# Stacked float32r products for a low rank term, one-step value ends and products of ones in a planned TensorE stream

## The chip, the cores and the metric

The kernel runs on one core of a Trainium2 chip. The metric is the time of one execution on the device, in microseconds (us). Three runs of the kernel before took 713.5, 714.14 and 715.22 us; the median is 714.14. The profile is of one further execution.

## The reference

Four sequences of 576 tokens go through three blocks, all in float32. Cut to what matters:

```
# 1: windowed attention, 8 heads of 64
scores = where(0 <= i-j < 128, q k^T/8 - slope_h |i-j|, -1e9);  x = softmax(scores) v   # (4, 576, 512)
# 2: low rank mixing of tokens, then a wide layer over channels
h = x^T @ U @ V                  # U: 576 x 32, V: 32 x 576, for each sequence
u = x + h^T
x = u + relu(u @ w_ch1) @ w_ch2  # 512 -> 2048 -> 512
# 3: gated unit
h = relu(x @ w_in);  a, v = halves of h (512 each)
v_n = (v - mean(v)) / sqrt(var(v) + 1e-6)
v_s = w_spatial @ v_n + b_spatial       # mixes the 576 tokens
out = (a * v_s) @ w_out
```

The inputs `U`, `V` and the weights are float64 in memory and are brought to float32 bit by bit in the kernel.

## The kernel before, in words

Nothing in the kernel is issued in the order of the source text. Every step is a `Task` with an engine (or several to choose from), an estimated cost, a due time and the buffer parts that it reads and writes. `Plan.run` lays all tasks out in a simulated time line eight times, each time with due times worked out backwards from the layout before, keeps the layout that ends first, and emits the instructions in that order. So the order on each engine's queue is fixed before the launch, and a changed cost or task anywhere may change the order everywhere. Buffers are slots of rings; two rings may name the same slot, and a later user of a slot waits for the earlier one. Semaphores come from these uses.

**Exact products.** TensorE multiplies float32r operands in one pass, float32 operands in two recorded passes. Where float32 accuracy is wanted at the float32r rate, an operand is split in a float32r high part and a float32r remainder, and a product becomes three: high by high, low by high, high by low. The wide layers use this (lines 545 to 547, 584 to 586, 885 to 887, 1421 to 1423 and others).

**Front.** The four sequences' attention comes first (`heads`, a task group for each pair of heads): scores (line 1044), maximum and bias on VectorE (1055), exponentials on ScalarE (1060), scaling on VectorE or GpSimd (1082), transposes (1090), products with the values (1128). Sequence 0 is scaled after the products (`plain`). Between these tasks the planner sets the first quarter of the wide layer (`early_group`, lines 545 to 586), as soon as its tokens are ready. `turn_over` (991) issues products of a 128 by 128 tile of ones (`hot`) before the first scores.

**Low rank term.** `turned` transposes a sequence's `u` (1155). `low_rank` mixes the tokens with `U` into a PSUM tile `t` whose strip of 32 partitions number `pair` holds the 32 mixed rows of that pair of heads (1171). A copy brings `t` to SBUF as `th`; then `up` makes, for each half of 288 tokens, one float32 product per pair on that pair's strip of 32 rows of the array: 32 rows of `th` against the same strip of `v32`, which holds `V` four times, one copy for each strip (1184). VectorE adds each result to `u` (1189). Sequence 0 does this in two calls of `low_rank` for two pairs each, the other sequences in one for all four.

**Values.** In the third block (`values_of`) the tokens are taken in tiles of 128, of which the first 64 tokens of two sequences b and b+1 share one (c = 0, in every even sequence). Its normalised rows must stand as two tiles `ends`, where rows 64i to 64i+63 belong to sequence i: `ends[0]` holds twice the first 32 tokens, `ends[1]` twice the next 32. Line 1476 normalises 32 rows at a time into each end and line 1479 doubles them on ScalarE. The edge operands of the token mixing (`value_forms`, 1506) read them, and the last product of each sum (1577) uses these. Line 1593 adds the sums.

## Time and profile before

| | |
|---|---|
| median of 3 runs | 714.14 us (713.5 to 715.22) |
| profiled execution | 713.79 us, of which the span is 712.0 us |
| TensorE products | 701.7 us busy (99%) |
| TensorE weight loads | 637.8 us (90%) |
| VectorE | 576.0 us (81%) |
| ScalarE | 394.0 us (55%) |
| GpSimd | 75.0 us (11%) |
| DMA | 98.48 MB, mean 138 GB/s |

The span is the time from the first to the last instruction of the profiled execution. Busy shares are means over stretches with different limits: attention fills about the first 180 us, the wide layer goes on to about 510 us, the gated unit takes the rest. In timelines of TensorE a row is a group of like instructions with its start, its length and, in brackets, the time that the engine stood idle before it and what ended that. In a table by stretches a row holds the stretch and its length, then the busy time of TensorE's products, its weight loads, VectorE, ScalarE and GpSimd with the number of instructions, then the granted clock (1.00 is the upper level, 2.4 GHz), the DMA engines' busy share and GB/s. A product's length includes the way through the array; how often products follow each other is read from their starts.

### The profile page before, as it was taken

The numbers are of one execution on the slowest core, as the hardware profiler recorded it, in microseconds if no ns is written. First come the engines' busy times: TensorE is split into PE (matmuls) and PEld (weight loads), VectorE is DVE, ScalarE is ACT, GpSimd is POOL, SyncE is SP. The second block draws the span as 40 slices with busy tenths as digits, with TensorE's granted clock in tenths as the row PEclk, the third lists the DMA queues.
The fourth block names the chain that finished last, engine by engine and source line by source line (L and its number), as shares of the span: only waits on it lengthen the run. The fifth ranks groups of instructions, "written<-read, shape, count | busy, mean of one in ns | idle before, by whom it ended". The sixth has DMA issues, their size and how long they took to land.

```text
span 712.0 us, 14829 instructions
## 1 busy us (share of the span) xinstructions
PE 701.7 (99%) x5434; PEld 637.8 (90%) x5434; DVE 576.0 (81%) x1637; ACT 394.0 (55%) x1082; POOL 75.0 (11%) x114
## 2 busy tenths in 40 slices
PE   8989999999999999999999999999999999999998
PEld 6767778778799999999999999999998898898896
DVE  6999996775597999999695998696589989859561
ACT  7878666564353655547253562544267566566352
POOL 2243330310400000000000000040010100100000
DMA  8865212210074166628475555447694202100102
GB/s 233 280 221 161 66 52 82 72 53 2 1 225 157 42 228 220 223 106 267 149 225 175 168 195 185 144 148 264 239 386 174 80 30 68 54 22 0 60 1 75
DMA packets 58799, 98.48 MB, mean 138 GB/s; under 512 B 8357, under 2 KB 38309, under 8 KB 58726
## 3 DMA queue, kind: packets, MB, share of 16 engines
q1 hardware_dynamic: 58437, 97.23, 41.2%
q8 instruction: 43, 0.70, 0.4%
q14 instruction: 31, 0.25, 0.1%
q10 hardware_dynamic: 288, 0.30, 0.1%
HBM read 67.67 MB, written 29.54 MB: 137 GB/s over the span
## 4 chain that ended last, share of the span: by engine, by line
PE 88%; DVE 7%; ACT 2%; DMA 1%; issue 1%; POOL 0%; SPq 0%; POOLq 0%; ACTq 0%
PE sc L586 8%; PE sc L584 8%; PE sc L585 8%; PE at L885 6%; PE at L886 6%; PE at L887 6%; PE at L1128 3%; PE sc L1044 2%; PE sc L1423 2%; PE sc L1421 2%; PE sc L1422 2%; PE at L1090 2%; PE at L1423 2%; PE at L1421 2%; PE at L1422 2%; PE acc L584 2%
## 5 line engine op out<-in xcount | busy, mean ns | idle before, releaser
L584 PE MATMUL sc<-h,wa 128*128 128x384 f32 (+1 forms) x328 | 110.6, 337 | 0.0
L585 PE MATMUL sc<-h,wa 128*128 128x384 f32 (+1 forms) x328 | 110.5, 337 | 0.0
L586 PE MATMUL sc<-hl,wa 128*128 128x384 f32 x320 | 108.7, 340 | 0.0
L1060 ACT ACTIVATE p<-p,nmax 128x192 f32<-128x192 f32 (+2 forms) x144 | 61.5, 431 | 10.2 <-DVE nmax L1055 10.0
L584 PEld LDWEIGHTS sc<-h,wa 128*128 128x128 f32 x328 | 61.6, 188 | 0.3
L585 PEld LDWEIGHTS sc<-h,wa 128*128 128x128 f32 x328 | 61.5, 187 | 0.3
L933 DVE TENSOR_TENSOR y<-sc,y 128x384 f32<-128x384 f32 (+1 forms) x96 | 40.7, 450 | 25.6 <-PE sc L586 25.3
L885 PE MATMUL at<-xd,wa 128*128 128x384 f32 x180 | 60.9, 338 | 0.0
L886 PE MATMUL at<-xd,wa 128*128 128x384 f32 x180 | 60.8, 338 | 0.0
L887 PE MATMUL at<-xd,wa 128*128 128x384 f32 x180 | 60.8, 338 | 0.0
L586 PEld LDWEIGHTS sc<-hl,wa 128*128 128x128 f32 x320 | 60.1, 188 | 0.0
L1055 DVE CUSTOM_DVE_ANT_0 p<-sc,bias 128x192 f32<-128x192 f32 (+2 forms) x144 | 40.3, 328 | 12.7 <-PE sc L1044 12.4
L905 ACT COPY c<-at 128x384 f32<-128x384 f32 x54 | 25.8, 478 | 39.2 <-PE at L887 38.9
L416 ACT CAST wa<-st 128x256 fp32r<-128x256 f32 (+1 forms) x62 | 28.1, 475 | 25.2 <-DVE st L465 13.1
L897 ACT ACTIVATE h<-c 128x384 fp32r<-128x384 f32 x54 | 28.4, 526 | 19.7 <-DVE c L892 19.5
L892 DVE TENSOR_TENSOR c<-at,c 128x384 f32<-128x384 f32 x54 | 29.8, 551 | 8.2 <-PE at L887 4.9
L885 PEld LDWEIGHTS at<-xd,wa 128*128 128x128 f32 x180 | 33.8, 188 | 0.0
L886 PEld LDWEIGHTS at<-xd,wa 128*128 128x128 f32 x180 | 33.8, 188 | 0.0
L887 PEld LDWEIGHTS at<-xd,wa 128*128 128x128 f32 x180 | 33.8, 188 | 0.0
L1044 PE MATMUL sc<-kr,qr 64*64 64x192 f32 (+2 forms) x576 | 31.7, 319 | 1.2 <-DMA qr<-in_qT 0.7
L1090 PE MATMUL at<-ident,p 128*128 128x128 f32 x208 | 31.1, 281 | 1.5 <-DVE p L1082 1.4
L1090 PEld LDWEIGHTS at<-ident,p 128*128 128x128 f32 x208 | 23.0, 140 | 10.4 <-issue 3.3
(407 smaller groups left out, 2007.7 us busy)
## 6 DMA issues: line engine op xcount, KB each, us to landing
wa<-in_w SPq DMA_DIRECT2D x32, 512.0 KB, 4.3
xd<-formsa SPq DMA_DIRECT2D x24, 192.0 KB, 3.0
qr<-in_qT SPq DMA_DIRECT2D x15, 288.0 KB, 3.3
kr<-in_kT SPq DMA_DIRECT2D x15, 288.0 KB, 4.0
vr<-in_v SPq DMA_DIRECT2D x16, 256.0 KB, 4.3
raw<-in_w_in SPq DMA_DIRECT2D x8, 512.0 KB, 3.9
kepts<-raw SPq DMA_DIRECT2D x14, 288.0 KB, 2.1
out<-h SPq DMA_DIRECT2D x15, 256.0 KB, 2.0
```

Source lines behind the costliest of these rows:

```text
L584: nc.tensor.matmul(o, wt[:, 0, 0, c], hh[:, j], start=i == 0 and x == 0, stop=False, skip_group_check=True)
L585: nc.tensor.matmul(o, wt[:, 1, 0, c], hh[:, j], start=False, stop=False, skip_group_check=True)
L586: nc.tensor.matmul(o, wt[:, 0, 0, c], hl[:, j], start=False, stop=i == len(wts) - 1, skip_group_check=True)
L885: nc.tensor.matmul(o.ap(), wh()[:, k], xh.ap(), start=start and k == 0, stop=False, skip_group_check=True)
L886: nc.tensor.matmul(o.ap(), wl()[:, k], xh.ap(), start=False, stop=False, skip_group_check=True)
L887: nc.tensor.matmul(o.ap(), wh()[:, k], xl.ap(), start=False, stop=k == 1, skip_group_check=True)
L892: P.add("DVE", dve(N3), lambda: nc.vector.tensor_tensor(out=out.ap(), in0=ps_.ap(), in1=sb.ap(), op=ALU.add), r=[ps_, sb], w=[out], prio=0)
L933: P.add("DVE", dve(m), lambda acc=acc, dst=dst, s=s, m=m, o=o: nc.vector.tensor_tensor(out=dst[:, s : s + m], in0=acc[:, 0, o : o + m], in ...
L1044: nc.tensor.matmul(s[o : o + 64, c0 : c0 + k1 - k0], qr[d, 64 * t : 64 * t + 64], kr[d, k0:k1], start=True, stop=True, skip_group_check=True)
L1055: nc.vector.tensor_tensor_reduce(out=o(), in0=s[:, c0 : c0 + nk], in1=bias_t[:, pair, t % 2, 192 - nk :], scale=-0.125, scalar=BIG, op0=AL ...
L1060: nc.scalar.activation(out=o(), in_=o(), func=AF.Exp, scale=-1.0, bias=nmax[:, sl, t : t + 1], accum_out=sums[:, sl, t : t + 1])
L1090: P.add("PE", 0.109, lambda pt=pt, n_=n_, s0=s0: nc.tensor.transpose(pt[:, n_ - s0], p[:, n_ * 128 : n_ * 128 + 128], ident), r=[p.part(t) ...
```

## The change

Three things change, and the planner runs anew on all tasks.

1. For the sequences 1 to 3 the low rank products are stacked. A zeroed tile `four` holds, for each pair of heads, three strips of 32 rows: the float32r high part of the mixed rows twice and the remainder once. `v32r` holds the high part of `V` in its rows 0 to 63 and its remainder in rows 64 to 127, each twice. One float32r product over 128 rows then gives high by high, low by high and high by low together. Sequence 0 stays as it was. `v32`, `th` and the new temporary `v4h` move to slots of the output `y[1]`.
2. The shared tile of the values is normalised in one step in place, and three copies for each sequence bring the rows to their places, on ScalarE or VectorE.
3. Tasks of TensorE can carry a `fill`: a product of ones into the task's own PSUM buffer. Where the chosen layout starts such a task between 34 and 60 us after a gap, up to three fills are issued ahead of it, one for each 0.25 us of the gap.

```diff
+FILL = 0.25, 3, 34.0, 60.0
...
+        end = 0.0
         for t, t.eng, t.cost, t.emit, t.start in min(plans)[2]:
+            if t.eng == "PE":
+                for _ in range(min(FILL[1], int((t.start - end) / FILL[0])) if t.fill and FILL[2] < t.start < FILL[3] else 0):
+                    t.fill()
+                end = t.start + t.cost
             t.emit()
...
+    def ones_into(o):
+
+        return lambda: nc.tensor.matmul(o(), hot.ap(), hot.ap(), start=True, stop=True, skip_group_check=True)
...
-    r_xt, r_th = Ring(in_att, "xt", 2), Ring(in_att, "th", 2)
+    early_y = lambda i, shape, dtype: Ring(in_left, "y", 0, more=[f"y_{i}"]).new(shape, dtype)
+    r_xt, r_th = Ring(in_att, "xt", 2), Ring(in_left, "y", 0, more=["y_5", "y_7"])
+    four = constant("four", [128, 4, 128], F32R)
+    P.add("POOL", 0.3, lambda: nc.gpsimd.memset(f32(four.ap()), 0.0), w=[four.part(pair) for pair in range(4)], prio=-1)
...
-    v32 = constant("v32", [128, S], F32)
+    v32, v32r = early_y(6, [128, S], F32), constant("v32", [128, S], F32R)
...
+        v4h = early_y(4, [128, n], F32R)
+        late = 90.0
+        P.add("ACT", act(n, 0.09), lambda: nc.scalar.copy(out=v4h.ap(), in_=v4[:, 0]), r=[v4], w=[v4h], prio=late)
+        minus(("DVE",), n, lambda: v4[:, 0].bitcast(F32R), lambda: v4[:, 0], lambda: f32(v4h.ap()), r=[v4h], w=[v4], prio=late)
+        for q in range(2):
+            for d, (src, t) in enumerate(((lambda: f32(v4h.ap()), v4h), (lambda: v4[:, 0], v4))):
+                P.dma(64, n, lambda q=q, d=d, src=src: nc.sync.dma_start(
+                    out=f32(v32r[64 * d : 64 * d + 64, q * n : q * n + n]), in_=src()[64 * q : 64 * q + 64]),
+                    r=[t], w=[v32r.part((q, d))], prio=late)
...
-        t, th = tp.new([128, 128], F32), r_th.new([128, 128], F32)
+        t, th = tp.new([128, 128], F32), None if b else r_th.new([128, 128], F32)
...
+        if b:
+            strip = lambda g: slice(32 * g, 32 * g + 32)
+            for pair in pairs:
+                part, low = four.part(pair), 0 if pair == 1 else 1
+                def highs(copy_, pair=pair):
+                    for to in (pair, 2 if pair < 2 else 0):
+                        copy_(out=four[strip(to), pair], in_=t[strip(pair)])
+
+                P.either([("ACT", 0.47, lambda highs=highs: highs(nc.scalar.copy)), ("DVE", 0.5, lambda highs=highs: highs(nc.vector.tensor_copy))],
+                         r=[t], w=[part], prio=p0 + 0.05)
+                P.add("DVE", 0.3, lambda pair=pair, low=low: nc.vector.tensor_tensor(
+                    out=four[strip(low), pair], in0=t[strip(pair)], in1=f32(four[strip(pair), pair]), op=ALU.subtract), r=[t], w=[part], prio=p0 + 0.05, lat=0.8)
+            for s0 in (0, 288):
+                sl = slice(s0, s0 + 288)
+                for pair in pairs:
+                    o, ub = (sc, tp)[pair % 2].new([128, 288], F32), u[b][pair]
+                    P.add("PE", mm(288), lambda pair=pair, o=o, sl=sl: nc.tensor.matmul(o.ap(), four[:, pair], v32r[:, sl], start=True, stop=True),
+                          r=[four.part(pair)] + list(v32r.parts.values()), w=[o], prio=p0 + 0.1)
+                    P.add("DVE", dve(288), lambda o=o, ub=ub, sl=sl: nc.vector.tensor_tensor(
+                        out=ub[:, sl], in0=o.ap(), in1=ub[:, sl], op=ALU.add),
+                        r=[o], w=[ub.part(0), ub.part(1), ub], prio=p0 + 0.2)
+            return
...
-            r = (r_hr if c else r_ho).new([128, 512], F32)
+            r = (r_hr if c else r_hv).new([128, 512], F32)
...
-                ends = stage["ends"] = [r_hv.new([128, 512], F32) for _ in range(2)]
+                other = r_hv.new([128, 512], F32)
+                stage["ends"] = [r, other]
+                sides = [r.part((i, h)) for i in range(2) for h in range(2)]
+                P.add("DVE", dve2(512) + 0.13, lambda r=r, mv=mv, rs=rs: nc.vector.tensor_scalar(
+                    out=r.ap(), in0=r.ap(), scalar1=mv[:, 0:1], scalar2=rs[:, :1], op0=ALU.subtract, op1=ALU.mult),
+                    r=[mv, rs], w=both + sides, port=True, prio=base)
                 for i in range(2):
...
+                    low, high = slice(64 * i, 64 * i + 32), slice(64 * i + 32, 64 * i + 64)
+                    mine, theirs = [[e.part((i, h)) for h in range(2)] for e in (r, other)]
+                    for to in (high, low):
+                        copy(BOTH, 512, lambda to=to, other=other: other[to], lambda r=r, high=high: r[high], None, r=mine, w=theirs, prio=base)
+                    copy(BOTH, 512, lambda r=r, high=high: r[high], lambda r=r, low=low: r[low], None, w=mine, prio=base)
```

The tasks that carry a fill are the first products of `early_group`, the scores, the transposes (1090, 1155), the products of `spread` (1101), of `pv` (1128) and of the mix (1171).

## Rows read from the trace of the kernel before

**Rows 1.** Table by stretches: busy us of each engine (instructions), granted clock, DMA

```profile
34.00:60.00 26.00, 23.02 (x320) 16.47 (x317) 25.51 (x94) 20.23 (x69) 9.79 (x11) 1.00 0.61 201
86.00:190.00 104.00, 103.76 (x1285) 79.50 (x1285) 73.15 (x284) 59.52 (x205) 20.97 (x32) 1.00 0.15 45
...
630.00:640.00 10.00, 10.00 (x77) 10.00 (x77) 8.41 (x20) 7.52 (x21) 0.00 (x0) 1.00 0.01 2
```

**Rows 2.** TensorE's waits: who waited for whom, us, times, longest

```profile
PE at L1090 <- DVE p L1082: 1.4, 2, 1.0
...
PE f L1574 <- DVE y L1593: 0.9, 1, 0.9
```

**Rows 3.** Timeline of TensorE (start, length), sequence 1, then sequence 3

```profile
87.34 0.50 PE L584 MATMUL acc<-h,wa 128*128 128x512 f32 x1
...
88.63 0.39 PE L586 MATMUL acc<-h,wa 128*128 128x512 f32 x1
88.94 0.51 PE L1184 MATMUL sc<-v,th 32*128 32x288 f32 x1
...
88.97 0.51 PE L1184 MATMUL at<-v,th 32*128 32x288 f32 x1
...
89.64 0.50 PE L584 MATMUL acc<-h,wa 128*128 128x512 f32 x1
89.98 0.40 PE L585 MATMUL acc<-h,wa 128*128 128x512 f32 x1
...
90.91 0.40 PE L586 MATMUL acc<-h,wa 128*128 128x512 f32 x1
...
91.93 0.55 PE L1090 MATMUL at<-ident,p 128*128 128x128 f32 x3
...
183.23 0.40 PE L586 MATMUL acc<-h,wa 128*128 128x512 f32 x1
...
184.59 0.39 PE L585 MATMUL acc<-h,wa 128*128 128x512 f32 x1
```

**Rows 4.** Timeline of TensorE in the last stage

```profile
524.25 0.39 PE L1423 MATMUL at<-wa,fg 128*128 128x512 f32 x1
524.48 0.29 PE L1528 MATMUL at<-u,wa 128*128 128x288 f32 x1
524.61 0.30 PE L1529 MATMUL at<-u,wa 128*128 128x288 f32 x1
```

**Rows 5.** Groups by form, ScalarE, then VectorE: busy us, mean ns

```profile
L416 ACT COPY th<-at 64x128 f32<-64x128 f32 x2 | 0.5, 260 | 1.3 <-PE at L1171 1.3
...
L602 DVE TENSOR_TENSOR raw<-raw 128x288 fp32r<-128x288 f32 x14 | 6.3, 448 | 0.0
...
L594 DVE TENSOR_TENSOR y<-acc,u 128x128 f32<-128x128 f32 x2 | 0.6, 290 | 2.2 <-PE acc L586 2.2
```

**Rows 6.** Timeline of all engines behind the last low rank call

```profile
191.88 0.34 PE L545 MATMUL at<-xd,wa 128*128 128x384 f32 x1
```

**Rows 7.** Timeline of SP's queue from 34 us

```profile
34.85 1.86 SPq L446 DMA_DIRECT2D wa<-in_w  x3
48.87 0.33 SPq L1008 DMA_DIRECT2D qr<-in_qT  x1
```

**Rows 8.** Timeline of TensorE at the start

```profile
1.04 2.50 PE L991 MATMUL f<-hot 128*128 128x128 f32 x10 [1.04 <-DVE hot L950]
```

**Rows 9.** Three lines: count, ns (min/median/max), first and last start

```profile
L1476 DVE TENSOR_SCALAR h<-h,mv,rs x8: 527/534/549, 528.3 to 615.0; 32x512 f32<-32x512 f32 x8
...
L1465 DVE TENSOR_SCALAR h<-h,mv,rs x16: 530/546/549, 516.7 to 663.8; 128x512 f32<-128x512 f32 x16
...
L1479 ACT COPY h<-h x8: 611/618/620, 528.9 to 617.7; 32x512 f32<-32x512 f32 x8
```

**Rows 10.** Timeline of VectorE, then of TensorE, gated unit

```profile
543.97 0.54 DVE L1476 TENSOR_SCALAR h<-h,mv,rs 32x512 f32<-32x512 f32 x1
...
547.21 0.40 PE L1574 MATMUL f<-raw,x 128*128 128x288 f32 x1 [0.94 <-DVE y L1593]
```

More of the change, by code (lines that the diff above doesn't have):

```diff
@@ L140 @@
 class Task:
-    __slots__ = ("eng", "cost", "emit", "ways", "prio", "deps", "succ", "left", "before", "start", "lat", "port", "mode")
+    __slots__ = ("eng", "cost", "emit", "ways", "prio", "deps", "succ", "left", "before", "start", "lat", "port", "mode", "fill")
 PASSES = 8
+FILL = 0.25, 3, 34.0, 60.0
 class Plan:
@@ L157, in add, with either @@
         return self.either([(eng, cost, emit)], **kw)
-    def either(self, ways, r=(), w=(), prio=0, lat=0.0, deps=(), port=False, mode=None):
+    def either(self, ways, r=(), w=(), prio=0, lat=0.0, deps=(), port=False, mode=None, fill=None):
         t = Task()
-        t.ways, t.prio, t.lat, t.port, t.mode = {way[0]: way for way in ways}, prio, lat, port, mode
+        t.ways, t.prio, t.lat, t.port, t.mode, t.fill = {way[0]: way for way in ways}, prio, lat, port, mode, fill
         d = set(deps)
@@ L564, in early_group @@
                 P.add("PE", 12 * mm(n), lambda f1=f1, j=j, wt=wt: first_of(f1[:, j], wt, hs, ls),
-                      r=[p for x in hs + ls for p in x[2]] + [wt.part(0), wt.part(1)], w=[f1], prio=prio)
+                      r=[p for x in hs + ls for p in x[2]] + [wt.part(0), wt.part(1)], w=[f1], prio=prio,
+                      fill=ones_into(lambda f1=f1, j=j: f1[:, j, :128]))
             hh, hl = r_h.new([128, w, n], F32R), r_h.new([128, w, n], F32R)
@@ L1047, in heads @@
             scored = [P.add("PE", 4 * max(sum(64 * min(t + 1, 3) for _, t, _ in tiles if t % 2 == o) for o in range(2)) / 2400 + 0.1,
-                  score, r=[x.part(c) for x in (qr, kr) for c in CUTS if c < 64 * tiles[-1][1] + 64], w=list(s.values()), deps=filled, prio=p0 + 1, mode="quarters")]
+                  score, r=[x.part(c) for x in (qr, kr) for c in CUTS if c < 64 * tiles[-1][1] + 64], w=list(s.values()), deps=filled, prio=p0 + 1, mode="quarters",
+                  fill=ones_into(lambda s=next(iter(s.values())): s[:, :128]))]
             for _, t, _ in tiles:
@@ L1102, in spread @@
                                              start=True, stop=True, skip_group_check=True)
-                P.add("PE", 320 * 4 / 2400 + 0.1, spread, r=[dg, ones], w=rs, prio=p0 + 4.5, mode="quarters")
+                P.add("PE", 320 * 4 / 2400 + 0.1, spread, r=[dg, ones], w=rs, prio=p0 + 4.5, mode="quarters", fill=ones_into(lambda: rs[0][:, :2]))
                 r = r_d.new([128, 9, D], F32)
@@ L1130, in pv @@
                                 started.add((e, j))
-            P.add("PE", 13 * 64 * 4 / 2400 + 0.2, pv, r=[vr, last] + [x.part(g) for g in range(4)], w=os_, prio=p0 + 8, mode="quarters")
+            P.add("PE", 13 * 64 * 4 / 2400 + 0.2, pv, r=[vr, last] + [x.part(g) for g in range(4)], w=os_, prio=p0 + 8, mode="quarters",
+                  fill=ones_into(lambda: os_[0][:, :2]))
             if plain:
@@ L1174, in low_rank @@
         P.add("PE", 5 * 4 * 128 / 2400 + 0.1, mix, r=[u32] + [xts[h].part(c) for h in {p // 2 for p in pairs} for c in (0, 2, 4)],
-              w=[t], prio=p0, mode="quarters")
+              w=[t], prio=p0, mode="quarters", fill=ones_into(t.ap))
+        if b:
[19 more added lines that the diff above has]
+            return
         copy(engines("t", "ACT"), 128, lambda: th[rows], lambda: t[rows], PSUM, r=[t], w=[th], prio=p0 + 0.05)
@@ L1469, in values_of @@
             else:
-                ends = stage["ends"] = [r_hv.new([128, 512], F32) for _ in range(2)]
-                for i in range(2):
-                    to, next_ = slice(64 * i, 64 * i + 32), slice(64 * i + 32, 64 * i + 64)
-                    for j, e in enumerate(ends):
-                        at = slice(64 * i + 32 * j, 64 * i + 32 * j + 32)
-                        parts = [e.part((i, h)) for h in range(2)]
-                        P.add("DVE", dve2(512) + 0.13, lambda r=r, mv=mv, rs=rs, e=e, at=at, to=to: nc.vector.tensor_scalar(
-                            out=e[to], in0=r[at], scalar1=mv[at, 0:1], scalar2=rs[at, :1], op0=ALU.subtract, op1=ALU.mult),
-                            r=[mv, rs, *both], w=parts, port=True, prio=base)
-                        P.add("ACT", act(512, 0.09), lambda e=e, to=to, next_=next_: nc.scalar.copy(out=e[next_], in_=e[to]), w=parts, prio=base)
+                other = r_hv.new([128, 512], F32)
[4 more added lines that the diff above has]
+                    r=[mv, rs], w=both + sides, port=True, prio=base)
+                for i in range(2):
+                    low, high = slice(64 * i, 64 * i + 32), slice(64 * i + 32, 64 * i + 64)
[3 more added lines that the diff above has]
+                    copy(BOTH, 512, lambda r=r, high=high: r[high], lambda r=r, low=low: r[low], None, w=mine, prio=base)
         stage[b] = (sums, vn)
```

4 lines of the change are left out of this document (2 added, 2 removed).

## Prediction

> **What bounds the kernel now.** I read four views, in this order. The page gives the busy shares: TensorE is busy for 701.7 of 712.0 us, VectorE for 81%, ScalarE for 55%. So an edit pays if it takes time from TensorE's own stream, or one of its waits, which are 10.3 us together. The table by stretches says where the waits lie: 2.98 us of 26 in the stretch from 34 to 60 us, where VectorE is busy for 25.5 of 26; only 0.24 us of 104 from 86 to 190, where the second to fourth sequences pass; the granted clock is 1.00 throughout, the level of 2.4 GHz [rows 1]. The reader is to see that the low rank products of the later sequences (line 1184) lie in a stretch in which TensorE never waits, so that every microsecond taken from them is one off the span. The list of TensorE's waits names one that the value ends can touch: 0.9 us of L1574 for a sum on VectorE [rows 2]. The timelines then give the price of a single step.
>
> **Products of the low rank term.** Each of sequences 1 to 3 makes two calls of `up`: four float32 products, each on a strip of 32 rows. The four start together (88.94 to 88.97) and each is recorded as two passes one behind the other. After the last float32r product before it (start 88.63) the second one behind it starts at 89.98. That is 1.35 us, where three starts of such products back to back are 0.46 apart (0.23 each, as from 524.25 to 524.48) [rows 3, 4]. The call thus costs 0.89 us. The two passes take 0.70 of it, from 88.94 to 89.64; the rest are the edges: the start after a full-height product comes at 0.31 instead of 0.23, and the first product behind the call takes 0.34 until the next instead of 0.23. Six calls stand in the trace. Four lie between float32r products and span 1.35, 1.37, 1.64 and 1.36 us (the last from 183.23 to 184.59 [rows 3]); less 0.46 these are 0.89, 0.91, 1.18 (0.24 of it a wait right behind the call) and 0.90. Two are followed by a transpose, 90.91 to 91.93 and the like, 1.02 and 1.03 us; less 0.23 these are 0.79 and 0.80. Together 5.47 us.
>
> The change puts 24 full-height float32r products of 288 columns in their place. Products of that form stand in the last stage: 77 start in 10 us [rows 1], 0.130 each, and one that follows a product of 512 columns costs no edge (524.25, 524.48, 524.61) [rows 4]. 24 by 0.130 are 3.12 us. The difference is 2.35 us less. Bounds: if every new product paid an edge of 0.11, 24 by 0.24 are 5.76, a loss of 0.3; at 288 columns per 0.12 us, the pure rate of 2.4 GHz, they take 2.88 and save 2.6 at most. I take 2.35, since the nearest rows are this very form in this very neighbourhood, other float32r products.
>
> Here a rule of the skill speaks against the edit. The four strip products overlap, as the starts within 0.03 us show [rows 3]. The Trainium skill (TensorEngine Tiling, Theoretical Speedup) promises up to 4 times the throughput for a contraction of at most 32, which the change gives up; by that the array would do the same work in both forms and the gain would be about nil. The same page (Tiling Modes, Key Properties) says that a change of mode drains TensorE; the longer starts at both ends of the call agree with that.
>
> **What feeds them.** Before, one ScalarE copy of the mixed tile led to the products. Now each of four pairs needs two copies of 32 by 128 from PSUM (0.26 us by the copies of 64 by 128) and one VectorE subtraction (0.29 by the 128 by 128 form) [rows 5]. If all eight copies queue on ScalarE, the last pair is ready about 8 x 0.26 + 0.29 - 0.27 = 2.1 us later than now. What hides it is the rest of the early group's work on TensorE. In the last sequence, the one with least to follow, L584 to L586 run without a wait from the end of the second call at 184.59 to 191.88, when L545 first needs the result [rows 3, 6]: 7.3 us that can be drawn ahead of the new products. ScalarE and VectorE have room there (59.5 and 73.2 us busy of 104 [rows 1]). Behind the waiting products on TensorE's queue stand those same L584 products, and behind these the accumulators of L594. Cost taken: 0; bounds 0 and 3 x 2.1 = 6.3 us.
>
> **Front stretch.** The split of V adds one ScalarE copy, one VectorE subtraction of 128 by 288 (0.45 [rows 5]) and four transfers on SP before sequence 1 needs them at 88 us. SP issues nothing between 36.7 and 48.87 us [rows 7], so the transfers get by. VectorE is full there, so the subtraction costs between 0 and 0.45; I take 0.2. The tiles moved into slots of `y[1]` are read before that output is first written; no wait. The zeroing of `four` runs on GpSimd at the start, beside the first loads: 0.
>
> The products of ones stand before TensorE tasks that the plan starts between 34 and 60 us, up to three each. Ten of the same kind at the start take 2.50 us, 0.25 each [rows 8]. Where the wait is for data (the longest, 1.4 us in two parts, is for VectorE's L1082 [rows 2]) they lie inside it and cost nothing. Where the chip has no wait at the place of the planned one, each costs 0.25 in front of the task, and VectorE and ScalarE get their operands that much later. They gain nothing: the clock is at its upper level already [rows 1]. Bounds: 0, and 12 of them uncovered, 3.0 us (the waits in the stretch could hold twelve); I take 0.2, near the lower end, since the trace has 2.98 us of waits there to put them in.
>
> **Ends of the values.** For the sequences 0 and 2 four VectorE steps of 32 by 512 (0.53 each) become one of 128 by 512 (0.55), and four ScalarE copies (0.62) become six that may go to either engine [rows 9]. VectorE is spared 1.6 us each time, less whatever copies it takes on. In sequence 0 two of the four old steps run at 543.97 (0.54) and in the same way at 545.25 (0.55), right ahead of the sums for which TensorE waits 0.94 us until 547.21 [rows 10]. Without them (1.09 us) the wait could go entirely; with copies put in their place it would stay. Half: -0.5, bounds -0.94 and 0. Late next are the edge rows: three copies in a row instead of one, 1.2 us longer. In sequence 2 there is no wait to win.
>
> **The sum.** -2.35 - 0.5 + 0.2 + 0.2 = -2.45 us on the profiled execution's 713.79 (712.0 of span and 1.8 around it), 711.3. That execution lies 0.35 below the median of the runs, 714.14; for the median I say 711.7. The planner sorts all tasks anew from changed costs, so any wait of today can grow or vanish; single waits are up to about 1 us, which I add to both sides.
>
> **The rivals.**
> - *The products gain nothing.* By what the strips share, or because the new products are scattered among transposes and scores and pay an edge each (0.11): the first term is 0 instead of -2.35 and the time is 714.0. For it: 24 products replace work whose pure streaming is no longer than theirs. Against it: the edges of 0.31 and 0.34 that stand around each call [rows 3].
> - *The strips come late* (the other side). After L1171 ScalarE makes the copies in order, with exponentials between them, and TensorE reaches the products before they are ready. Price up to 2.1 us a sequence; with two of three exposed, 4.2 - 2.45, 715.9. It decides from about 0.8 us a sequence on, where it eats the whole gain. For it: in sequence 1 only 1.6 us lie between the mix and the first call (L584 behind the mix starts at 87.34, the call at 88.94), less than the new chain takes [rows 3]. Against it: 7.3 us of other products even in the last sequence [rows 3, 6].
> - *More than the sum.* The wait at 547 goes whole, and the front loses a microsecond of its 2.98 as well: 714.14 - 2.35 - 0.94 - 1.0, 709.8. For it: VectorE is the releaser of both [rows 2]. Against it: the front gets more VectorE work, not less.
>
> **How the numbers follow.** Forecast 0.52 (its own range 710.5 to 712.9), no gain 0.24, late strips 0.11, more 0.13. What a measurement of this kernel can tell from no change is about 0.2%, 1.4 us, so faster means under 712.7: 0.50 of the first case and all of the last, 0.63. Within it: the no-gain case and the rest of the first, 0.26. Slower: the late strips, 0.11. The range from 709.3 to 714.4 leaves out most of the slower case and the tail of the last.
>
> **What would show it.** In the changed profile the strip products of sequences 1 to 3 (48 records, two to a product) should be gone, and in their place stand 24 products with starts 0.13 apart and no longer start before or behind them; TensorE's busy time should fall by about 2.3 us while its waits stay near 10. If the starts are 0.2 or more apart, the first rival holds. A wait of TensorE on ScalarE or VectorE for `four` would show the second. For the ends: fewer VectorE steps near 544, and L1574's wait shorter than 0.9. The ones should appear as products beside waits from 34 to 60 us, with the total of waiting and ones together no larger than 3 us. The prediction is wrong if TensorE's busy time outside the ones does not fall by 2 us, or if its waits from 34 to 190 us grow by over 1.5 us.

## The result, and the profile after

The changed kernel takes 719.02 us (median of 6 runs, 717.25 to 720.07), the kernel before 714.21 (6 runs, 713.5 to 715.47) in the same session: ratio 1.0066, 95% interval 1.0054 to 1.0078. It is 4.8 us slower; 711.7 was forecast. The profiled execution took 718.6 us, with a span of 716.7. Executions of one kernel fall in two groups by their mean granted clock: of 107 of the kernel before, 24 lie at 0.997 or 0.998, with a median of 715.2 us, and the rest, called "at full clock" below, at 0.999 or 1.00, with 714.0.

The table by stretches of the changed kernel answers to [rows 1], with the same columns:

```profile
34.00:60.00 26.00, 24.61 (x325) 18.34 (x323) 25.11 (x82) 20.55 (x66) 11.95 (x12) 1.00 0.62 194
86.00:190.00 104.00, 102.02 (x1259) 80.31 (x1257) 75.30 (x296) 59.46 (x205) 20.11 (x34) 1.00 0.16 47
630.00:640.00 10.00, 10.00 (x77) 10.00 (x76) 5.54 (x13) 6.03 (x14) 0.00 (x0) 1.00 0.07 26
```

The stretch in which TensorE had not waited (0.24 us of 104) now holds 1.98 us of waits. The list of TensorE's waits, beside [rows 2], names them (who waited for whom, us, times, longest):

```profile
PE at L1114 <- DVE nmax L1079: 1.4, 1, 1.4
PE acc L595 <- DVE y L605: 1.3, 2, 0.6
...
PE f L1623 <- DVE y L1642: 0.6, 1, 0.6
...
PE sc L1217 <- ACT wa L422: 0.6, 1, 0.6
PE at L896 <- ACT c L916: 0.5, 1, 0.5
```

L1217 are the new products, L595 the wide layer's behind them, L1623 the product behind the value ends (0.9 in [rows 2]). The first and the last row are new places: 32 us and 484 us, away from the edited steps.

The timeline of sequence 1 (answers to [rows 3]) shows the chain that feeds the products: mix, strip copies (L1207, ACT and DVE), subtractions (L1211), products. Rows of other work in between are left out:

```profile
88.95 1.30 PE L1196 MATMUL at<-xt,u 128*32 128x128 f32 x40
90.18 0.50 PE L595 MATMUL acc<-h,wa 128*128 128x512 f32 x1
90.32 0.52 ACT L1207 CAST four<-at 32x128 fp32r<-32x128 f32 x2 [1.78 <-PE at L1196]
90.87 0.60 DVE L1207 CAST four<-at 32x128 fp32r<-32x128 f32 x2 [0.43 <-ACT four L1207]
91.51 0.52 ACT L1207 CAST four<-at 32x128 fp32r<-32x128 f32 x2 [0.67 <-DVE four L1207]
92.06 0.62 DVE L1207 CAST four<-at 32x128 fp32r<-32x128 f32 x2 [0.59 <-ACT four L1207]
92.13 0.39 PE L597 MATMUL acc<-h,wa 128*128 128x512 f32 x1
92.69 1.24 DVE L1211 TENSOR_TENSOR four<-at,four 32x128 fp32r<-32x128 f32 x4
93.08 0.51 PE L1217 MATMUL sc<-v,four 128*128 128x288 f32 x2 [0.56 <-ACT wa L422]
93.44 0.37 PE L1217 MATMUL at<-v,four 128*128 128x288 f32 x1
93.66 0.40 PE L1217 MATMUL sc<-v,four 128*128 128x288 f32 x1
94.71 0.50 PE L595 MATMUL acc<-h,wa 128*128 128x512 f32 x1 [0.65 <-DVE y L605]
...
96.20 0.42 PE L1217 MATMUL at<-v,four 128*128 128x288 f32 x2
96.47 0.30 PE L1217 MATMUL sc<-v,four 128*128 128x288 f32 x1
96.60 0.29 PE L1217 MATMUL at<-v,four 128*128 128x288 f32 x1
96.73 0.40 PE L595 MATMUL acc<-h,wa 128*128 128x512 f32 x1
```

Three things are to be seen. The copies are spread over two engines, yet each waits for the other engine's (the brackets): 2.4 us in a row instead of 1.2 side by side. The first four products start at 93.08, 93.28, 93.44 and 93.66, about 0.2 us apart, since each new pair of heads waits for its subtraction, and these take 0.31 each; the later ones, whose operands lie ready, come 0.13 apart, as predicted. And VectorE, busy with the subtractions, frees the wide layer's accumulator late (0.65 us at 94.71). The row at 93.08 puts its wait down to ScalarE's L422; the wait that fits the edit is that for the first subtraction, which ends at 92.98.

The products of ones (8, in 16 records):

```profile
39.40 0.49 PE L563 MATMUL at<-hot 128*128 128x128 f32 x2
41.17 0.94 PE L563 MATMUL at<-hot 128*128 128x128 f32 x6 [0.62 <-ACT xt L422]
47.45 0.61 PE L563 MATMUL sc<-hot 128*128 128x128 f32 x4
48.79 0.71 PE L563 MATMUL f<-hot 128*128 128x128 f32 x4
```

The three at 41.17 stand behind the wait that they were to fill: they write the same PSUM buffer as the task they precede, so they wait for that buffer too (0.62 us, for ScalarE to read it out) and then run in front of the task. What they cost in the end is asked below (`no_ones`).

Three marks place the loss in the two profiled executions, the first two rows from before, the third from after:

```profile
86.11 1.30 PE L1171 MATMUL at<-xt,u 128*32 128x128 f32 x40
224.53 0.34 PE L885 MATMUL at<-xd,wa 128*128 128x384 f32 x1
...
228.30 0.34 PE L896 MATMUL at<-xd,wa 128*128 128x384 f32 x1
```

The mix of sequence 1 starts at 86.11 before and 88.95 after (+2.84); from there to the first product behind the wide layer's first quarter (L885, now L896, at 224.53 and 228.30) it is 138.42 and 139.35 (+0.93, though three wide-layer products, 0.7, moved ahead of the mix); from there to TensorE's end 484.38 and 485.01 (+0.63). These make 4.40 of the 4.7 us between the spans.

### The profile page after: what moved, and what is told of

Same layout as the page of the kernel before. It is cut to its first block, busy times and chain, and to the rows that moved or that the text cites. A ratio compares the mean times of both kernels' runs of the same rounds, so it can differ in the third digit from the quotient of the medians.

```text
span 716.7 us, 14893 instructions
## 1 busy us (share of the span) xinstructions
PE 704.9 (98%) x5426; PEld 643.4 (90%) x5426; DVE 577.0 (81%) x1645; ACT 398.8 (56%) x1100; POOL 79.7 (11%) x122
## 4 chain that ended last, share of the span: by engine, by line
PE 69%; DVE 3%; ACT 1%; DMA 0%; issue 0%; POOL 0%
PE sc L597 7%; PE sc L595 7%; PE sc L596 7%; PE at L896 6%; PE at L897 6%; PE at L898 6%; PE sc L1470 2%; PE sc L1468 2%; PE sc L1469 2%; PE at L1470 2%; PE at L1468 2%; PE at L1469 2%; PE sc L1623 1%; PE sc L1577 1%; PE at L552 1%; PE at L551 1%
## 5 line engine op out<-in xcount | busy, mean ns | idle before, releaser
L595 PE MATMUL sc<-h,wa 128*128 128x384 f32 (+1 forms) x328 | 110.8, 338 | 0.0
L595 PEld LDWEIGHTS sc<-h,wa 128*128 128x128 f32 x328 | 61.7, 188 | 0.5 <-DVE u L1219 0.2
L896 PE MATMUL at<-xd,wa 128*128 128x384 f32 x180 | 61.0, 339 | 0.5 <-ACT c L916 0.5
L422 ACT CAST wa<-st 128x256 fp32r<-128x256 f32 (+1 forms) x62 | 28.1, 475 | 27.7 <-DVE st L471 14.2
L896 PEld LDWEIGHTS at<-xd,wa 128*128 128x128 f32 x180 | 33.8, 188 | 0.9 <-ACT c L916 0.8
L1114 PE MATMUL at<-ident,p 128*128 128x128 f32 x208 | 30.3, 280 | 2.1 <-DVE nmax L1079 1.4
L1152 PEld LDWEIGHTS at<-ph,vr 128*64 128x64 f32 (+1 forms) x960 | 24.9, 135 | 7.6 <-issue 2.0
```

The lines of the kernel that those rows point to most:

```text
L595: nc.tensor.matmul(o, wt[:, 0, 0, c], hh[:, j], start=i == 0 and x == 0, stop=False, skip_group_check=True)
L896: nc.tensor.matmul(o.ap(), wh()[:, k], xh.ap(), start=start and k == 0, stop=False, skip_group_check=True)
L1114: P.add("PE", 0.109, lambda pt=pt, n_=n_, s0=s0: nc.tensor.transpose(pt[:, n_ - s0], p[:, n_ * 128 : n_ * 128 + 128], ident), r=[p.part(t) ...
```

## The experiments

Ratios are to runs of the kernel before in the same session, with a 95% interval behind them.

**1. The parts of the change.** `no_ones`: the changed kernel, same order.

```diff
-FILL = 0.25, 3, 34.0, 60.0
+FILL = 0.25, 0, 34.0, 60.0
```

> The changed kernel in the same order, without the 8 products of ones (16 records, 2.1 us of TensorE's time in its trace). Theory 'own work' (ones and late strips cost what they take): about 2 us less, 717. Theory 'order' (the new layout of the front is slower by itself, and the ones stand in waits that are there anyway): within 0.5 us of the changed kernel, 718.5 to 719.

717.43 us (717.14 to 717.92), ratio 1.0047 [1.0035, 1.0059]. That is 1.6 us less by the medians. But all 5 of these runs are at full clock, and of the changed kernel's 6 only two are (717.25 and 718.6; the median of the other four is 719.55). Against those two the difference is 0.5 us, and 0.3 against the five that they make with three of `own_tiles` (below), which has the same order and the same ones. The profiles put the ones' own price at nothing. The first row stands ahead of the first product of ones (39.40), the second is the mix of sequence 1, both from `no_ones`; the third is the first row's counterpart with ones:

```profile
30.87 0.55 PE L1114 MATMUL at<-ident,p 128*128 128x128 f32 x3 [1.33 <-DVE nmax L1079]
87.72 1.30 PE L1196 MATMUL at<-xt,u 128*32 128x128 f32 x40
...
32.11 0.55 PE L1114 MATMUL at<-ident,p 128*128 128x128 f32 x3 [1.36 <-DVE nmax L1079]
```

From L1114 to the mix it is 56.85 us without the ones and 56.84 with them (88.95 less 32.11). The 1.2 us between the two profiles stand ahead of the ones.

`ones_alone`: the kernel before, its order, ten products of ones by the same rule.

> The kernel before in its own order, with the ones alone: 10 products in its planned gaps from 34 to 60 us, 0.26 us each by the changed trace. Theory 'own work': up to 2.6 us more than before, 716.8. Theory 'order': the ones lie in waits, 714.2 to 714.7.

714.32 us, 1.0003 [0.9994, 1.0012]: they cost nothing that can be measured there. None of its 11 runs lies below full clock.

`ends_replanned`: the kernel before with the diff's value part (`values_of`) alone, planned anew.

> The kernel before with the value part of the change alone (one 128 by 512 step, six copies), sorted anew by the planner. Theory 'the products lose': the ends are worth what the wait behind them lost in the changed kernel, 0.94 to 0.57 us: 713.4 to 714.0. Rival 'the ends lose': 1 us or more above the kernel before, 715 and over, with a longer wait for the edge rows or for VectorE near 480 and 550 us.

714.59 us, 1.0008 [1.0000, 1.0017]. The wait behind the ends falls from 0.94 to 0.61, but a new one of 0.33 stands at 480 us (L885, for ScalarE's L905). The ends give nothing; by the interval they cost between 0 and 1.2 us.

`products_replanned`: the kernel before with the diff's product part (`low_rank`, `low_rank_weights`, `four`) alone, planned anew.

> The kernel before with the product part of the change alone (stacked float32r products, split of V, the tiles moved into slots of y), sorted anew by the planner; no ones, the value ends as before. Theory 'the products lose': the strips are built one behind the other, the 24 products come at 0.22 us each and TensorE waits for strips and sums around them, so most of the 3.5 us that the change lost without its ones is here: 716.5 to 717.5. Rival 'the front and the ends lose': the products cost about 1 us, 714.5 to 715.5, and the other 2 us lie in the changed ends or in a front that this kernel plans as well as the kernel before. My prediction's own term would give 711.6.

717.9 us (716.36 to 719.3), 1.0050 [1.0036, 1.0065]. Most of the loss is here, at full clock too (716.6 for three runs).

**2. Is it the chosen layout?** `second_layout` (the kernel before) and `after_second_layout` (the changed one):

```diff
-        for t, t.eng, t.cost, t.emit, t.start in min(plans)[2]:
+        for t, t.eng, t.cost, t.emit, t.start in sorted(plans)[1][2]:
```

> The kernel before with nothing changed but the planner's choice: the layout that ends second instead of the one that ends first, of the same eight. No work is added or taken. Theory 'order': layouts of nearly the same planned length differ on the chip by several us, so 716 to 719, with the loss before 90 us. Theory 'own work': the same as before within 0.7 us, 713.5 to 714.9.

713.74 us, 0.9995 [0.9987, 1.0004].

> The changed kernel with the second best of its eight layouts in place of the best: same tasks, another order. Theory 'the strips are late': every order builds the strips one behind the other, so the loss stays: 717 to 720, TensorE's products near 0.22 us each. Rival 'the chosen order is unlucky': 714 to 716.

719.81 us, 1.0078 [1.0065, 1.0091]. One other order of the same tasks changes little on either side.

**3. The strips.** `own_tiles`: the changed kernel with a tile of its own for each pair in place of the shared `four`, same order.

```diff
-    four = constant("four", [128, 4, 128], F32R)
+    four = [constant(f"four{pair}", [128, 128], F32R) for pair in range(4)]
```

> The changed kernel in the same order, but with a tile of its own for the strips of each pair instead of one shared tile. In the changed trace the copies for the four pairs run one after the other, though they are spread over ScalarE and VectorE. If that is from the shared tile, the chain of 3.6 us shrinks to about 2 and TensorE's waits around the new products (2.0 us in three sequences) go: 717 to 717.5. If something else ties them (the PSUM tile that all read), no change: 719. By theory 'order' the front (3.2 us behind at the second mix of sequence 0) stays as it is in both cases.

718.93 us, 1.0068 [1.0056, 1.0080]; the brackets of the copies are the same. The shared output is not what ties the engines. In its profile the wait at 32 us is missing and the mix of sequence 1 stands at 86.68, against 88.95 in the changed kernel with the same order of instructions: over 2 us of the front differ from one execution to the next.

`no_strips`: the changed kernel, same order, without the feeding; the products read a tile of zeros.

```diff
-                    for to in (pair, 2 if pair < 2 else 0):
-                        copy_(out=four[strip(to), pair], in_=t[strip(pair)])
+                    pass
...
-                P.add("DVE", 0.3, lambda pair=pair, low=low: nc.vector.tensor_tensor(
-                    out=four[strip(low), pair], in0=t[strip(pair)], in1=f32(four[strip(pair), pair]), op=ALU.subtract), r=[t], w=[part], prio=p0 + 0.05, lat=0.8)
+                P.add("DVE", 0.3, lambda: None, r=[t], w=[part], prio=p0 + 0.05, lat=0.8)
```

> The changed kernel in its own order with the feeding of the products left out: no strip copies and no subtractions, the products of sequences 1 to 3 read the zeroed tile (their term is left out of the result). Theory 'the strips are late': the 24 products, which took 0.222 us each in the changed kernel, run at 0.13 (3.1 instead of 5.3), and the waits of 0.65 and 0.62 at 94.7 and 142.0 go: 719.0 - 2.2 - 1.2 to 1.9, 715.0 to 715.8. What is then left above 714, 1 to 2 us, is the front and the ends. Rival 'the products themselves are dear': they stay above 0.2 each and the time above 717.5.

715.9 us (714.17 to 718.47), 1.0022 [1.0011, 1.0034]. From the mix of sequence 1 to L896 it is 136.26 instead of 139.35: feeding the strips costs 3.1 us there. The 24 products take 4.07 instead of 5.33 (0.170 each; some still wait for PSUM).

`strips_from_sbuf`: the changed kernel, same order, one copy of `t` to SBUF more; the strips are made from that.

```diff
+                    flat.append(Buf(hot.ring, hot.slot, None, [128, 128], F32))
+                    copy_(out=flat[0].ap(), in_=t.ap())
...
-                        copy_(out=four[strip(to), pair], in_=t[strip(pair)])
+                        copy_(out=four[strip(to), pair], in_=mixed(copy_)[strip(pair)])
```

> The changed kernel in its own order; in sequences 1 to 3 the mixed tile goes from PSUM to SBUF by one copy of 128 by 128, and the strip copies and subtractions read it there. Theory 'readers of one PSUM tile take turns': ScalarE and VectorE then copy side by side, the chain from the mix to the last strip, 3.6 us, falls to about 0.3 + 1.2 + 0.4 = 1.9, the products come close together and the time is 717 to 717.8. Rival 'the copies take turns for another reason': the chain is 0.3 us longer than now, 719 to 720.

715.71 us (714.96 to 717.88), 1.0024 [1.0015, 1.0034]: a copy was added and 3.3 us are gained by the medians. Part of that is clock: 4 of these 12 runs lie below full clock, 4 of 6 of the changed kernel. Among runs at full clock it is 2.5 us (715.4 for eight, 717.9 for two), among the others 2.4. In the profile the stretch from the mix of sequence 1 to L896 is 137.31 instead of 139.35, 2.0 us less. Rows of sequence 1, with rows of other work left out, and L896:

```profile
88.30 1.30 PE L1196 MATMUL at<-xt,u 128*32 128x128 f32 x40
89.67 0.27 ACT L1208 COPY hot<-at 128x128 f32<-128x128 f32 x1 [1.79 <-PE at L1196]
89.97 1.26 ACT L1215 CAST four<-hot 32x128 fp32r<-32x128 f32 x4
89.97 0.95 DVE L1215 CAST four<-hot 32x128 fp32r<-32x128 f32 x4 [0.18 <-ACT hot L1208]
90.95 1.22 DVE L1219 TENSOR_TENSOR four<-hot,four 32x128 fp32r<-32x128 f32 x4
91.72 0.43 PE L1225 MATMUL sc<-v,four 128*128 128x288 f32 x2
...
225.61 0.34 PE L896 MATMUL at<-xd,wa 128*128 128x384 f32 x1
```

Both engines start at 89.97 and copy side by side; from the end of the mix to the last strip it is 2.6 us instead of 3.7. The only thing that changed is where they read: it was the common PSUM tile that made them take turns. The Trainium skill (PSUM — Partial Sum Buffer, PSUM bank collisions raise a hardware error) says that two engines may not touch one PSUM bank in the same 32 partitions at once, reads against reads included, so that a program must order them. The brackets of the changed kernel agree as to the bank; its copies of different pairs read different 32 partitions and were ordered too, so here the order is coarser than that: it goes by the tile or by its bank, and no run here tells which.

**4. The products in the old order.** `stacked_kept_order` puts the stacked products where the old calls stood, all eight copies on ScalarE from PSUM.

```diff
+            for pair in pairs:
+                for to in (pair, 2 if pair < 2 else 0):
+                    nc.scalar.copy(out=four(pair)[strip(to)], in_=t[strip(pair)])
...
+                        nc.tensor.matmul(o.ap(), four(pair), stacked[2][:, sl], start=True, stop=True)
+                        continue
```

> The kernel before in its own order of all instructions; only the old strip products of sequences 1 to 3 are replaced in place by the 24 stacked float32r products, their eight strip copies stand on ScalarE where the one copy stood, the subtractions on VectorE where the first call stood, V is split during sequence 1. Theory 'the form is cheap, its strips are late': the products run 0.13 us apart in a row once they begin (24 by 0.13 against 5.5, -2.35 us), but the strips need 8 copies of 0.26 and a subtraction of 0.29, 2.4 us against 1.6 us between mix and first call, plus what VectorE and ScalarE have in front of it: a wait of TensorE of 1 to 2 us per sequence right ahead of the first product: 714 to 717. Rival 'the new order is to blame': nothing of the loss is left, 712 to 713.5. A third, 'the form is dear': the products are 0.2 us apart even in a row.

725.93 us, 1.0161 [1.0148, 1.0175], the worst of all. Its two calls in sequence 2:

```profile
142.70 0.59 DVE L1211 TENSOR_TENSOR v<-at,v 32x128 fp32r<-32x128 f32 x2 [1.35 <-ACT more L1198]
143.03 0.40 PE L1212 MATMUL sc<-v,v 128*128 128x288 f32 x1 [1.69 <-DVE v L1211]
143.44 0.37 PE L1212 MATMUL at<-v,v 128*128 128x288 f32 x1
143.76 0.37 PE L1212 MATMUL sc<-v,more 128*128 128x288 f32 x1
144.08 0.37 PE L1212 MATMUL at<-v,more 128*128 128x288 f32 x1
144.29 0.39 PE L584 MATMUL acc<-h,wa 128*128 128x512 f32 x1
...
145.67 0.30 PE L1212 MATMUL sc<-v,v 128*128 128x288 f32 x1
145.80 0.29 PE L1212 MATMUL at<-v,v 128*128 128x288 f32 x1
145.93 0.29 PE L1212 MATMUL sc<-v,more 128*128 128x288 f32 x1
146.07 0.29 PE L1212 MATMUL at<-v,more 128*128 128x288 f32 x1
```

The same instruction comes every 0.32 to 0.41 us when each operand is made just ahead of it, by subtractions that take about 0.3 each, and every 0.13 when all lie ready. A wait that the profile counts (1.69) is only part of the price: the slow pace behind it counts as busy.

`stacked_sbuf_kept`: the same with strips from SBUF on both engines and V split where it is loaded; `stacked_sbuf_kept_ones` adds the ten ones.

```diff
+                for pair in (0, 2, 1, 3):
+                    for to in (pair, 2 if pair < 2 else 0):
+                        (nc.vector.tensor_copy if pair % 2 else nc.scalar.copy)(out=four(pair)[strip(to)], in_=th[strip(pair)])
```

> The kernel before in its own order; only the old products of sequences 1 to 3 become the 24 stacked ones. The mixed tile is copied to SBUF as before, the strips are copied from there (two pairs on ScalarE, two on VectorE), V is split where it is loaded, its four transfers stand at the start of sequence 1. Theory 'the product term was right but for the strips': 24 by 0.13 to 0.17 are 3.1 to 4.1 instead of 5.47, less a wait of up to 0.4 a sequence for the third and fourth strip, plus up to 0.5 in the front: 712.6 to 714.0. Rival 'the edges were no gain': 714.2 or more, the mixes of sequences 1 to 3 as far apart as before (46.7 and 46.75) or farther.

725.41 us, 1.0148 [1.0134, 1.0163], 11 us above the theory's range. In the old order VectorE has other work between copies and subtractions, and TensorE waits 1.3, 2.3 and 0.9 us in the three sequences; 2.4 more are mine, at 28 us, where the split of V blocks VectorE until V's transfers have read the tile. The table by stretches of this kernel shows what a long wait does beyond itself:

```profile
138.00:141.00 3.00, 2.51 (x45) 1.52 (x43) 2.48 (x8) 2.52 (x10) 1.36 (x3) 1.00 0.48 175
141.00:144.00 3.00, 1.22 (x4) 1.16 (x5) 2.78 (x9) 0.23 (x1) 1.15 (x3) 0.75 0.10 25
144.00:146.00 2.00, 2.00 (x6) 1.62 (x6) 2.00 (x7) 0.00 (x0) 0.00 (x0) 0.52 0.15 38
146.00:148.00 2.00, 2.00 (x16) 1.51 (x15) 1.44 (x5) 0.60 (x2) 0.00 (x0) 1.00 0.20 52
```

The wait of 2.27 us ends at 142.78; the granted clock falls to half, the level of 1.2 GHz, at its end, and stays there until about 146, with TensorE fully busy at half pace.

> The kernel of stacked_sbuf_kept with the ten products of ones in the waits of the front. Theory 'the ones hold the granted clock in the waits of the front, at about their own price': none or one of its executions below 1.00 of clock, where 12 of 69 of the kernel before are, and the median within 0.4 us of the kernel without them. Rival 'the ones do nothing to the clock': as many executions below 1.00 as without them.

723.67 us, 1.0132 [1.0117, 1.0146]. All 4 runs lie below full clock, as all 4 without the ones do. In its profile the clock falls at the long waits of the later sequences, so the run says nothing on the ones.

`rows_kept_order`: float32r products on the old strips of 32 rows, three for each pair and half, one copy and one subtraction, V split on VectorE in sequence 1. `rows_split_on_gpsimd` moves that split 15 us later and to GpSimd.

```diff
+                    for k, (x, v) in enumerate(((th, high), (th, low), (tl, high))):
+                        for pair, o in zip(pairs, outs):
+                            nc.tensor.matmul(o.ap(), x[d], v[d], start=k == 0, stop=k == 2, skip_group_check=True)
```

> The kernel before in its own order; the strip products of sequences 1 to 3 become float32r products on the same 32-row strips: three for each pair and half (high by high, high by low, low by high), four pairs side by side, fed by one copy and one subtraction of 128 by 128; V is split into two tiles in sequence 1. If four strips run side by side in this form too, a call is three passes of 0.13 instead of two of 0.35, 0.39 against 0.70: 6 by 0.31, 1.9 us less, minus up to 0.3 us a sequence for the subtraction: 711.5 to 713. If the strips take turns in this form, a call is 12 by 0.13, 1.56 us: 719. Theory 'the chain of strips costs': this kernel has no chain, so no wait for strips longer than 0.3 us.

715.19 us (714.14 to 718.31), 1.0020 [1.0008, 1.0033]. Four strips do run side by side in this form, three passes in 0.60 us instead of two in 0.70, but the three sequences gain nothing: 138.82 for the stretch that took 138.42. No wait for strips is left. The mix of sequence 1 stands at 88.12 instead of 86.11, but this profile is of an execution below full clock, so how much of that is the split of V is open.

> The float32r products on 32-row strips in the order of the kernel before, with the split of V moved about 15 us later and its subtraction from VectorE to GpSimd. Theory 'the split hurt the full front, the calls gain a little': the mix of sequence 1 stands at 86.1 to 86.4 again instead of 88.1, the calls save 0.1 each: 713.3 to 714.0. Rival 'the calls gain nothing and the added subtraction costs': 714.3 to 715.

718.57 us, 1.0060 [1.0048, 1.0072], far above both theories. A new wait of 2.5 us for VectorE stands at 67 us, right behind the split, and the mix of sequence 1 starts at 91.73.

**5. The change mended.** `products_sbuf_replanned`: the product part with the copy to SBUF as a task that the planner knows; `products_sbuf_ones` adds the planned ones, `products_sbuf_second` takes the second layout, `change_sbuf_replanned` is the whole change so mended.

```diff
+            flat = hot.ring.new([128, 128], F32)
+            copy(BOTH, 128, flat.ap, t.ap, PSUM, r=[t], w=[flat], prio=p0 + 0.05)
```

> The product part alone, with the copy to SBUF as a task of its own that the planner knows, sorted anew; no ones, value ends as before. Theory 'the tie of the readers was the loss, what is left is the new front': 717.9 less the 3.3 us that the copy to SBUF gave the changed kernel, 714.3 to 715.3, with its second mix of sequence 0 still 1 to 2 us later than 38.9. Rival 'without the tie the new order is as good as the old one': 712.5 to 713.8.

714.73 us (714.11 to 716.7), 1.0013 [1.0004, 1.0023]: 3.2 us below `products_replanned`, 2.0 among runs at full clock. The 24 products take 3.77 us, 0.157 each, but 1.5 us of waits for VectorE stand in the same stretch. The plan is a new one as well: only 69 wide-layer products stand ahead of the mix of sequence 1, which starts at 85.17, where `products_replanned` has 75 and the kernel before 72. The stretch from there to L885 takes 139.25 us against 139.35, with six products (1.4 us) more in it: about 1.5 us of the gain lie there, and the rest in a front of another order.

> products_sbuf_replanned with its eight planned products of ones, the same order otherwise. 4 of its 12 executions had a clock below 1.00 and were 1.9 us longer. Theory 'the ones hold the clock': at most 1 of 12 below 1.00, time 714.3 to 714.9. Rival 'the ones do nothing, they only cost': as many below 1.00, 715 to 716.5.

714.9 us, 1.0011 [1.0003, 1.0020]; 0 of 11 runs below full clock against 4 of 12 without the ones, whose full-clock median is 714.6. In the changed kernel, with ones as well, 4 of 6 lie below, so ones in the front are not enough to hold the clock.

> products_sbuf_replanned with the second best of its eight layouts. If the chosen layout of the front is what is left of the loss, another may be the version that beats the kernel before: 712.5 to 713.8. If the stacked form itself has nothing left to win: 714.0 to 716.

716.3 us, 1.0033 [1.0020, 1.0045]. With as many wide-layer products ahead of the mix of sequence 1 as in the kernel before (72), its stretch to L885 takes 137.78 instead of 138.42: there the stacked form gains 0.6 us. It loses more in the front, where that mix starts at 88.47 instead of 86.11 in this profile.

> The whole change with one thing mended: the mixed tile goes to SBUF by a copy that the planner knows, the strips are built from there, and the planner sorts anew. Theory 'the tie of the readers was most of the loss, the ends and the ones are the rest': the product part alone came to 714.7 so; the ends add 0.4 (as alone) and the ones up to 1 us in the places that this plan finds: 714.7 to 716.2. Rival 'the parts do not add': the new plan brings a stall or a fall of the clock of its own, 717 and over, or loses one, below 714.

715.24 us, 1.0017 [1.0008, 1.0026]: 3.8 us below the changed kernel, 2.7 at full clock, by one added copy, the costs that the planner is given for the strips, and the plan that follows. No version of the products that was run beats the kernel before.

## Why the prediction was wrong

**The step that failed** is "What feeds them", with its "Cost taken: 0; bounds 0 and 3 x 2.1 = 6.3 us". Measured: 3.1 us in the profiles (`no_strips`), of which 2.0 go when the strips are read from SBUF (`strips_from_sbuf`). I had weighed eight copies in a queue on ScalarE, one subtraction behind them, and 7.3 us of products to draw ahead of the new ones. Both halves were wrong. The copies were spread over two engines and took turns on one PSUM tile, so they needed 2.4 us all the same, and all four subtractions (1.24 us) came behind them: 3.7 us from the end of the mix to the last strip (90.25 to 93.93), where my bound allowed 2.4. And what may be drawn ahead is not what is: the order is fixed from planned costs, and with those (0.47 or 0.5 for a pair's copies, side by side) the plan put only nine products of the wide layer, 2.3 us (90.18 to 92.52), in between. My rival "The strips come late" was this mechanism, at 0.11; it decided, as it said, from 0.8 us a sequence on, and its time, 715.9, was too low by what the front and the ends lost besides. Of the 7.3 us between the forecast for the profiled execution (711.3) and its time, this term is the largest with 3.1; the front gives 1.7 (less the 0.7 of displaced products), the stretch from L896 to the end 1.1 and the product term 0.9, together 6.8. The rest lies outside the three marks.

**The product term**, -2.35, had the right sign and was too large. Fed for nothing, the stretch falls by 2.16, of which 0.7 is displaced work: about -1.5. The count of 24 by 0.130 held only where operands and PSUM lay ready (0.170 each over all, in `no_strips`); in the changed kernel they took 0.222, 5.33 us instead of 3.12. Much of the edges in my 5.47 was real: the wide layer's own products take 1.0 less than before, beyond the displaced ones.

**The rival "The products gain nothing"** (714.0) is near what is left when the strips come in time: mended, the stacked form ends at 714.7, and three float32r passes on the old strips gain nothing either. Only in the stretch of `products_sbuf_second` is a gain to be seen, the 0.6 us above.

**The front**: +0.2 taken for the split of V, +0.2 for the ones; measured +2.84 in the profiled execution. Of this, 1.69 stands already at the first mix (27.78 before, 29.47 after), 1.36 is the wait at 32 us, and from there to the mix of sequence 1 the changed kernel loses nothing, though the three displaced products stand in it. Neither part belongs to the order of instructions alone: `own_tiles`, with the same order and the same ones, has its first mix at 28.49, no wait at 32 us, and is 0.57 behind at the mix of sequence 1. So the 0.2 for the ones, which I took from bounds of 0 to 3.0, held in the profiles: their wait for the buffer and their time behind it are made good before 88 us. What makes the start of the front later in some executions was not found. Of five profiles that share the front's order, ones apart, `own_tiles` has no wait at 32 us and the others 1.06 to 1.80. `no_strips` shows it as waiting for nothing that the profile knows:

```profile
32.14 0.55 PE L1114 MATMUL at<-ident,p 128*128 128x128 f32 x3 [1.80 <-issue]
```

In all five an instruction queue (q8 on the changed kernel's page: 43 packets, 0.70 MB), taken to be TensorE's, brings blocks of 16 KB, and the block of that time starts at 25.63 where there is no wait and at 28.22 to 29.73 where there is one, which then ends 2.4 to 2.8 us later. That the late block is the cause is argued from these times; no run moved it. In `products_replanned` the clock is 0.83 from 30 to 40 us, behind such a wait of 2.2 us, and in `no_strips` it falls to half at 33.7, behind its 1.80: in both, ahead of any product that the change feeds and of any product of ones.

**The ends**: -0.5 taken; `ends_replanned` measures +0.3 by the medians, with an interval that reaches down to 0, and +0.4 in the profile from L885 to the end. In the changed kernel the wait named fell by 0.37 (0.94 to 0.57), near what I took, but 0.53 came back at 484 us. Why the new plan makes ScalarE late there was not followed.

**The signs.** TensorE's busy time outside the ones was to fall by 2 us; it rose from 701.7 to 704.9 with 2.1 of ones in it. The new starts came 0.22 apart on the mean, which by my list was a sign of the first rival, though here it comes from the late strips; the wait for `four` is there. But the waits from 34 to 190 us did not grow by 1.5 together, as I had put it (3.69 before, 3.38 after): from 86 on they grew from 0.24 to 1.98, from 34 to 60 they fell from 2.98 to 1.39, where ones now run. The sign should have been put on the later stretch alone.

## What to carry to other kernels

Before spreading copies over two engines, look at what they read: from one PSUM tile they took turns here, and one copy to SBUF first paid for itself more than twice (2.0 us in the profile for three copies of 0.27). Price a new product by the instruction that feeds it, not by its own rate: operands made just ahead of it set its pace, and the profile counts that as busy. A filler product that needs the buffer that a wait is for runs behind the wait and not in it. And before a difference of medians is put down to an edit, compare executions at the same granted clock, and look whether the two traces part ahead of the edit: most of the 1.6 us of the ones and about 1 of the 3.3 us of the strips went that way.

## What the hardware showed that I had not expected

- Reads of one PSUM tile by ScalarE and VectorE came strictly in turn, even of different strips, each released by the other engine's (the brackets at 90.87, 91.51 and 92.06); the same reads from SBUF started together (89.97).
- One float32r product of 288 columns came every 0.13 us with its operand ready, every 0.32 to 0.41 with the operand made just before it by subtractions of about 0.3.
- A wait of 2.27 us was followed by some 3 us at half clock (0.52 from 144 to 146), in a sequence that took 50.1 us from mix to mix instead of 46.75, more than the wait's length longer.
- A wait of 1.06 to 1.80 us of TensorE at 32 us stood in four profiles of one order of instructions and not in the fifth.
